# The length-64 stage of a Fourier filter as four 64x64 tiles, with VectorE adding and subtracting mirrored inputs

## The chip, the cores and the metric

The kernel runs on one core of one Trainium2 chip. The metric is the device time of one execution in microseconds (us), median of several runs. The core's engines are TensorE (PE in the profile, its weight loads PEld), VectorE (DVE), ScalarE (ACT), GpSimd (POOL) and SyncE (SP), which here only issues DMAs. All data are float32.

## The reference

```python
def _attn_ref(x, filt_r, filt_i):            # x: (8, 3008, 256), filters: (1505, 256)
    X = np.fft.rfft(x, axis=1)
    F = (filt_r + 1j * filt_i)[None, :, :]
    Y = X * F
    return np.fft.irfft(Y, n=x.shape[1], axis=1).astype(np.float32)

def _moe_ref(x, w_tok1, w_tok2, w_ch1, w_ch2):   # d_tok 256, d_ch 1536
    xt = x.transpose(0, 2, 1)
    h = np.maximum(xt @ w_tok1, 0.0) @ w_tok2
    u = x + h.transpose(0, 2, 1)
    h2 = np.maximum(u @ w_ch1, 0.0) @ w_ch2
    return (u + h2).astype(np.float32)
```

The second function is applied to what the first returns. Each of the 8 batches goes through the filter along its 3008 positions and then through the mixer.

## The kernel before, in words

**The filter.** 3008 = 47 x 64. A transform along 3008 is done as transforms of length 64 (the "a" stage), then of length 47 with the multiplication by the filter and the way back (stages "b", "m", "i"). Positions are folded: one half of the 128 partitions holds the rows n1 = 23, 22, ... 0, the other half the mirrored rows 24 to 46 (and row 0 shifted by one), each with its 64 values n2. `a_unit` (L470) multiplies one chunk of two such row pairs, a 128x512 tile, by the 128x128 table `wa`: one matmul, which the profile shows as two records, since a float32 matmul is two instructions. ScalarE copies the result from the bank to a tile `t1`, and a DMA writes it to the DRAM buffer `z_tmp`. A batch has 12 such chunks. `x_load` (L439) brings the input chunks into the filter's tiles `filts`, which are free in this stage, six chunks ahead. `t2_load` (L527) reads z back, 2 DMAs for each of 16 steps c; `b_pair` (L577) and `bi_pair` (L591) are the two matmuls of a step, each through `four` (L569), which issues four matmuls on 64x64 tiles of the array, one on each quarter. Between them VectorE multiplies by the filter (L583) and joins the two halves (L588, L589). The result goes to `g_tmp` in DRAM.

**The groups.** Batches are filtered in `GROUPS` (0), (1, 2), (3, 4), (5, 6), (7). Group 0 runs ahead of everything in a form of its own. Each later group runs beside the mixer of the batches of the group before it.

**The mixer.** `mix` (L893) goes over 288 items: 8 batches, 6 column blocks m, 6 pairs of hidden blocks jp. The channel products are done with seven multiplications in place of eight (Strassen-Winograd), hence many sums on VectorE. The order of one item is written out by hand. On TensorE: `up_first` (4 matmuls, L783), part 0 of `down` for the item before (3, L817), `up_last` (3, L799), part 1 of `down` for the item before (4, L817). On VectorE: `up_middle`, `h_sums` of the item before, the two sums of `up_last`; all of these are recorded under L761. ScalarE copies `s` (L786) and applies ReLU (L804). At jp 3 and 4 come the quarters of the next block's U (L682, L704), at jp 0 to 2 the steps of `finish`, which read the banks `po`, turn the block and store it through GpSimd's queue (L864). At item 32 of each batch's 36 the token sums of the next batch are formed (L660), from `g_tmp` tiles that are loaded once that batch's filter is done.

**Where the filter's steps go.** `mix` yields three times per item: place 0 between part 0 of `down` and `up_last`, place 1 between `up_last` and part 1 of `down`, place 2 at the end. In the loop at L1045 a table says at which yields the filter goes a step on. For the groups from (3, 4) on, a step of stage "a" is due at places 1 and 2 of every item. Then a `b_pair` is due at jp 2 and 5. Every engine works through its own instructions in the order in which they are issued.

**Banks.** Two PSUM banks, `acc` and `b`, are shared by `a_unit`, `b_pair`, `bi_pair`, the quarters of U and the token sums; `free_bank` hands them out in turn, `two_banks` takes both.

Of the kernel before, what the change touches and what calls it, by code (L numbers as in the profile page):

```python
# [55 lines left out]
def _make_tables():  # L56
    n2 = np.arange(N2)
    one, two = slice(0, HALF), slice(HALF, P)
    wa = np.zeros((P, K2, 4))
    wai = np.zeros((K2, 4, P))  # L60
    for k2 in range(K2):
        th, th1 = (2 * np.pi * ((n * k2) % N2) / N2 for n in (n2, n2 + 1))
        c, s, c1, s1 = np.cos(th), np.sin(th), np.cos(th1), np.sin(th1)
        alt, alt1 = 1.0 - 2.0 * (n2 % 2), 2.0 * (n2 % 2) - 1.0
        rows = ((c, c1), (-s, s1), (-s, -s1), (c, -c1)) if k2 else ((c, c1), (alt, alt1), (c, -c1), (alt, -alt1))
        for g, (plus, minus) in enumerate(rows):
            wa[one, k2, g], wa[two, k2, g] = plus, minus
        wai[k2] = wa[:, k2].T * (2.0 if k2 else 1.0)
    wa, wai = wa.reshape(P, P), wai.reshape(P, P)

    n1 = A - 1 - np.arange(A)
    wb = np.zeros((4, A, K2, P))
    wi = np.zeros((P, K2, 4, A))
    for k2 in range(K2):
        for s in range(2 * A):
            if s < A:
                k, sign, q = k2 + 64 * s, 1.0, s
            else:
                j = s - A + 1
# [12 lines left out]
            for g, to, w in parts:  # L92
                wb[g, :, k2, to] = w * np.where(n1 == 0, 0.5, 1.0)
                wi[to, k2, g] = w * (1.0 if k2 or edge else 2.0) / N
    f = np.float32
    wi = wi.reshape(P, K2, KR)
    wa0 = wa.reshape(P, K2, 4).transpose(0, 2, 1).reshape(P, P)
    wbi0 = np.zeros((4, K2, K2, P + KR))
    wbi0[:, 0:A, :, 0:P] = wb
    wbi0 = wbi0.reshape(P, K2, P + KR)  # L100
    wbi0[:, :, P:] = wi
    wb = wb.reshape(KR, K2, P)
    wbi = np.zeros((P, K2 // KC, 4, HALF))
    for h in range(2):
        r, to = slice(h * HALF, h * HALF + KH), slice(h * HALF, (h + 1) * HALF)
        for i in range(KC):
            wbi[r, :, i] = wb[h * KH:(h + 1) * KH, i::KC, to]
            wbi[i * HALF:(i + 1) * HALF, :, 2 + h, 0:KH] = wi[to, i::KC, h * KH:(h + 1) * KH]
    return wa.astype(f), wa0.astype(f), wai.astype(f), wbi.astype(f), wbi0.astype(f)


@with_exitstack
def kernel(
# [10 lines left out]
):  # L124
    nc = tc.nc

    wa_np, wa0_np, wai_np, wbi_np, wbi0_np = _make_tables()
    wa_d = nc.inline_tensor(wa_np, name="wa_t").ap()
    wai_d = nc.inline_tensor(wai_np, name="wai_t").ap()
    ident_d = nc.inline_tensor(np.eye(P, dtype=np.float32), name="ident_t").ap()  # L130
    wait_d = nc.inline_tensor(np.ascontiguousarray(wai_np.T), name="wait_t").ap()
# [3 lines left out]


    place_of = {b: (g, i) for g, bs in enumerate(GROUPS) for i, b in enumerate(bs)}
    z_d, g_d = ([nc.dram_tensor("%s_tmp%d" % (what, g), (K2, KR, len(bs), D), FP32, kind="Internal").ap()
                 for g, bs in enumerate(GROUPS)] for what in "zg")

    w2_d = nc.dram_tensor("w2_tmp", (MT, P, 7, 256), FP32, kind="Internal").ap()

# [31 lines left out]
        return turn[0]  # L174

    wa = glob.tile([P, P], FP32, name="wa")
    wai = glob.tile([P, P], FP32, name="wai")
    wai_t = glob.tile([P, P], FP32, name="wai_t")
    ident = h1p.tile([P, P], FP32, tag="h1", name="ident")
# [256 lines left out]

    xs, ahead = {}, []

    def x_load(b, c, i, queue=None):  # L439

        where, tag = ((t3p, "t3"), (tp, "t"), (vp, "v"), (up, "u"), (t1p, "t1"), (t2p, "t2"), (wbp, "wb"))[c // 2 if b == 0 else 6]
        xc, dc = (2 * XC, D // 2) if b == 0 else (XC, D)
        d0, c = divmod(c, A // xc)
        j = i - XB if b in GROUPS[1] else i
        if b and j >= 0:
            j %= XF
            t = filts[j // 2][:, j % 2]
        else:
            t = where.tile([P, xc, dc], FP32, tag=tag, name="x")

        def rows(n1, ap):
            xb = x[b]
            return bass.AP(tensor=xb.tensor, offset=xb.offset + n1 * D + d0 * dc, ap=ap + [[1, dc]])

        for h in range(2):
            n = xc - 1 if h and (c + 1) * xc == A else xc
            q = queue or (nc.gpsimd if b == 0 and h else nc.sync)
            q.dma_start(t[h * HALF:(h + 1) * HALF, 0:n, :],
                        rows(A + c * xc if h else A - 1 - c * xc, [[N1 * D, N2], [D if h else -D, n]]))
            if n < xc:  # L460

                q.dma_start(t[HALF:P - 1, n, :], rows(N1, [[N1 * D, N2 - 1]]))
                q.dma_start(t[P - 1:P, n, :], rows(0, [[N1 * D, 1]]))
        xs[b, c + d0 * (A // xc)] = t

    def rows_of(t_d, b):
        g, i = place_of[b]
        return t_d[g].rearrange("k (g a) b d -> (k g) a b d", a=A)[:, :, i, :]

    def a_unit(b, c):  # L470
        ps = bank(free_bank())
        nc.tensor.matmul(ps, wa0 if b == 0 else wa, xs.pop((b, c)).rearrange("p a d -> p (a d)"), start=True, stop=True)  # L472
        if b == 0:
            d0, c = divmod(c, NXC // 2)
            nc.scalar.copy(out=turned[:, ts(c, 2 * XC), ds(d0 * P, P)], in_=ps.rearrange("p (a d) -> p a d", d=P))
            return
        t1 = t1p.tile([P, XC, D], FP32, tag="t1", name="t1")
        nc.scalar.copy(out=t1.rearrange("p a d -> p (a d)"), in_=ps)
        (nc.scalar if b in GROUPS[1] else nc.sync).dma_start(rows_of(z_d, b)[:, ts(c, XC), :], t1)

    def dft(bs):
        first = bs[0] == 0
        nb = len(bs)
        todo = [(b, c) for b in bs for c in range(NXC)]
        wbs = {}

        def table_load(c):
# [12 lines left out]

        def more(n, queue=None):
            for i, u in to_load[0:n]:
                x_load(*u, i, queue)
            del to_load[0:n]

        more(NXC if first else XB if bs == GROUPS[1] else XF)
        if bs == GROUPS[1]:
            ahead.append(more)
        if not first:
            yield "a"  # L510
        for i, u in enumerate(todo):
            if first and i in (0, 2):
                w_load(i // 2)
            if first and i in (6, 8):
# [12 lines left out]
        def t2_load(c):  # L527
            if first:
                return
            t2s[c] = t2p.tile([P, KC, nb, D], FP32, tag="t2", name="t2")  # L530
            for h in range(2):
                nc.sync.dma_start(t2s[c][ds(h * HALF, KH)],
                                  z_d[place_of[bs[0]][0]][ts(c, KC), ts(h, KH)].rearrange("k r b d -> r k b d"))

        def b_unit(k):
            ps = bank("pg").rearrange("p (b d) -> p b d", b=2)[:, 0:nb, :]
# [29 lines left out]

        def four(outs, stat, mov):  # L569
            for i in range(2):  # L570
                for j in range(2):
                    nc.tensor.matmul(outs(i, j), stat(i, j), mov(i, j), start=True, stop=True)  # L572

        def both(half, n=HALF):
            return slice(half * HALF, half * HALF + n)

        def b_pair(c):  # L577
            pss, wb, t2 = two_banks(), wbs[c], t2s[c]
            four(lambda h, i: pss[h][both(i)], lambda h, i: wb[both(h, KH), i], lambda h, i: t2[both(h, KH), i])
            where = (p1p, p2p)  # L580
            for h in range(2):
                prods[c, h] = where[h].tile([P, 2, nb, D], FP32, tag="p%d" % (h + 1), name="p%d" % (h + 1))
# [7 lines left out]

        def bi_pair(c):  # L591
            pss, wb, p = two_banks(), wbs[c], prods.pop((c, 0))
            four(lambda i, h: pss[i][both(h)], lambda i, h: wb[both(i), 2 + h], lambda i, h: p[both(i), h])
            t3 = t3p.tile([P, KC, nb, D], FP32, tag="t3", name="t3")
            for i in range(KC):
                by_block(t3[:, i], pss[i])
            for h in range(2):
                nc.sync.dma_start(g_d[place_of[bs[0]][0]][ts(c, KC), ts(h, KH)].rearrange("k r b d -> r k b d"),
                                    t3[both(h, KH)])

        for c in range(FB):
            if not first:
# [373 lines left out]
    with tc.manual_schedule():  # L976
# [6 lines left out]
        for i, _ in enumerate(dft(GROUPS[0])):  # L983
# [4 lines left out]
            if i < NXC:  # L988
                if i in (1, 3, 5, 7, 9):
                    start()  # L990
                if i == NXC - 1:
                    copies()
                    for t, src in ((wa, wa_d), (wai, wai_d), (ident, ident_d)):
                        nc.scalar.dma_start(t, src)
            elif k >= 0:
                if k == K2 - 5:
# [48 lines left out]
        for b, i, place in mix(next_ready):  # L1045
# [8 lines left out]
                continue  # L1054
            jp = i % JP
            if coming in "aw":
                due = group == 0 or place > 0
            elif group:
                due = (jp, place) in {"b": ((5, 1), (2, 1)), "m": ((0, 0), (3, 0)), "i": ((1, 0), (3, 2))}[coming]
            else:  # L1060
# [34 lines left out]
```

## Time and profile before

| | us |
|---|---|
| median of 3 runs | 2509.74 (2509.21 to 2513.75) |
| the profiled execution | 2507.99 |
| its span | 2506.2 |

| group of instructions | count | mean ns |
|---|---|---|
| L472 matmul of stage "a", 128*128, 128x512 | 164 | 592 |
| L572 matmul of `four`, 64*64, 64x512 | 384 | 624 |
| L817, L783, L799 matmuls of the mixer, 128x256 | 6,720 | 379 to 389 |
| L588, L589 VectorE sums, SBUF to SBUF, 128x512 | 96 | 688 to 695 |
| L583 VectorE product with the filter, 128x1024 | 96 | 1210 |
| L478 ScalarE copy of z, 128x512 | 84 | 574 to 582 |

The page gives each engine's busy time and share of the span, the chain of work that ended last, and groups of instructions by line with their mean length. [...] matmuls overlap, so what one costs is the distance from its start to the next one's start. The timeline lists instructions in order of time, merged where they are alike; "x2" is the number of records, and a bracket gives the idle time of the engine before the line and what ended it.

### The profile page before, as it was taken

The page shows a single profiled execution, that of the slowest core. Times are in us where ns is not written, and L with a number is a line of the kernel's source. Part 1 is how long each engine was busy: PE and PEld are TensorE (multiplying, and loading weights), DVE is VectorE, ACT ScalarE, POOL GpSimd, SP SyncE. Part 2 cuts the span into 40 slices and gives each one's busy share as a digit, 9 for nine tenths or more (in the row PEclk, how much of TensorE's full clock was granted, in tenths as well). Part 3 has the DMA queues.
Part 4 walks back from the last instruction along what each step waited for, and adds up shares of the span by engine and source line. Part 5 has one row for each costly group of instructions (what it writes and reads, how often), then busy time and mean ns, then how long its engine had stood idle before and what let it go on. Part 6 is the DMA issues. An engine that isn't in the chain of part 4 may idle for free.

```text
span 2506.2 us, 33323 instructions
## 1 busy us (share of the span) xinstructions
PE 2434.7 (97%) x11716; PEld 1982.6 (79%) x11716; DVE 1811.4 (72%) x3344; ACT 681.6 (27%) x1348; POOL 601.2 (24%) x1086
## 2 busy tenths in 40 slices
PE   7978999999999999999999999999999999999997
PEld 4656776977788777888778877898888888898887
DVE  7786878566785878565785788756786678757776
ACT  5633322132221222223221222213222222212221
POOL 6573332112111211211121112111212111212121
PEclk8999999999999999999999999999999999999999
DMA  9974444354332331235332222314222122201100
GB/s 220 256 211 116 130 124 137 98 162 133 99 85 53 81 82 49 87 115 160 101 88 67 79 73 69 102 51 129 76 85 74 47 71 66 63 24 28 39 16 18
DMA packets 172479, 235.97 MB, mean 94 GB/s; under 512 B 32386, under 2 KB 122742, under 8 KB 172312
## 3 DMA queue, kind: packets, MB, share of 16 engines
q1 hardware_dynamic: 127848, 175.53, 24.8%
q0 software_dynamic: 33376, 48.46, 7.7%
q10 hardware_dynamic: 11088, 9.85, 1.3%
q8 instruction: 93, 1.52, 0.3%
q14 instruction: 74, 0.61, 0.1%
HBM read 156.49 MB, written 77.22 MB: 93 GB/s over the span
## 4 chain that ended last, share of the span: by engine, by line
PE 82%; DVE 12%; issue 2%; DMA 2%; ACT 1%; DVEq 0%; SPq 0%; ACTq 0%; POOL 0%; POOLq 0%
PE ps_po L817 29%; PE ps_pg L783 17%; PE ps_pg L799 12%; PE ps_b L660 3%; PE ps_acc L660 3%; PE ps_b L572 3%; DVE t L761 3%; PE ps_b L704 3%; PE ps_acc L704 2%; DVE p L583 2%; DVE hh L761 2%; PE ps_b L682 2%; PE ps_acc L682 2%; DVE s L761 1%; PE ps_b L472 1%
## 5 line engine op out<-in xcount | busy, mean ns | idle before, releaser
L864 POOL DMA_DIRECT2D out_dram<-r x757 | 412.5, 553 | 1607.5 <-ACT hh L804 1332.3
L761 DVE TENSOR_TENSOR hh<-ps_pg,s 128x512 f32<-128x512 f32 (+3 forms) x864 | 482.5, 586 | 431.3 <-ACT s L786 428.0
L804 ACT ACTIVATE hh<-hh 128x512 f32<-128x512 f32 (+1 forms) x576 | 347.9, 621 | 983.0 <-DVE hh L761 983.0
L817 PE MATMUL ps_po<-t,wc 128*128 128x256 f32 (+1 forms) x2304 | 543.5, 379 | 3.9 <-DVE t L761 3.1
L817 PEld LDWEIGHTS ps_po<-t,wc 128*128 128x128 f32 x2304 | 428.8, 190 | 121.7 <-DVE t L761 33.8
L783 PE MATMUL ps_pg<-v,wc 128*128 128x256 f32 (+1 forms) x1728 | 415.1, 376 | 2.7 <-DVE v L761 2.1
L817 PE MATMUL ps_po<-hh,wc 128*128 128x256 f32 (+1 forms) x1728 | 413.7, 375 | 0.2 <-ACT hh L804 0.2
L783 PEld LDWEIGHTS ps_pg<-v,wc 128*128 128x128 f32 x1728 | 327.7, 191 | 44.3 <-DVE v L761 5.9
L817 PEld LDWEIGHTS ps_po<-hh,wc 128*128 128x128 f32 x1728 | 328.9, 191 | 38.0 <-ACT hh L804 0.5
L799 PE MATMUL ps_pg<-u,wc 128*128 128x256 f32 (+1 forms) x1152 | 295.7, 379 | 5.0 <-DVE hh L761 5.0
L799 PEld LDWEIGHTS ps_pg<-u,wc 128*128 128x128 f32 x1152 | 215.3, 190 | 63.0 <-DVE hh L761 29.0
L761 DVE TENSOR_TENSOR t<-t,hh 128x256 f32<-128x256 f32 (+1 forms) x576 | 246.6, 428 | 19.8
L761 DVE TENSOR_TENSOR s<-ps_pg,hh 128x512 f32<-128x512 f32 (+1 forms) x288 | 196.1, 681 | 30.7 <-DVE hh L761 0.9
L761 DVE TENSOR_TENSOR t<-hh 128x512 f32<-128x512 f32 (+1 forms) x288 | 193.7, 673 | 0.6 <-ACT hh L804 0.6
L783 PE MATMUL ps_pg<-u,wc 128*128 128x256 f32 (+1 forms) x576 | 173.9, 384 | 13.5 <-DVE hh L761 13.5
L786 ACT COPY s<-ps_pg 128x256 f32<-128x256 f32 (+1 forms) x288 | 106.0, 368 | 284.1 <-PE ps_pg L783 282.2
L799 PE MATMUL ps_pg<-v,wc 128*128 128x256 f32 (+1 forms) x576 | 168.7, 375 | 0.0
L783 PEld LDWEIGHTS ps_pg<-u,wc 128*128 128x128 f32 x576 | 105.7, 190 | 64.1 <-DVE hh L761 36.5
L799 PEld LDWEIGHTS ps_pg<-v,wc 128*128 128x128 f32 x576 | 109.3, 190 | 12.5
L761 DVE TENSOR_TENSOR u<-ps_b,u 128x512 f32<-128x512 f32 (+3 forms) x107 | 61.7, 577 | 69.7 <-PE ps_b L704 65.0
L761 DVE TENSOR_TENSOR u<-ps_acc,u 128x512 f32<-128x512 f32 (+3 forms) x103 | 58.9, 572 | 57.2 <-PE ps_acc L704 52.0
L660 PE MATMUL ps_b<-t,w 128*128 128x256 f32 x384 | 83.9, 380 | 5.3 <-DVE p L583 4.7
(135 smaller groups left out, 2435.8 us busy)
## 6 DMA issues: line engine op xcount, KB each, us to landing
w<-w_tmp SPq DMA_DIRECT2D x35, 896.0 KB
out_dram<-r POOLq DMA_DIRECT2D x698, 32.0 KB, 2.6
t<-g_tmp SPq DMA_DIRECT2D x42, 512.0 KB
filt<-in_x_dram SPq DMA_DIRECT2D x145, 128.0 KB
t<-z_tmp SPq DMA_DIRECT2D x96, 192.0 KB
g_tmp<-t SPq DMA_DIRECT2D x96, 192.0 KB
z_tmp<-t SPq DMA_DIRECT2D x60, 256.0 KB
wb<-wbi_t SPq DMA_DIRECT2D x64, 128.0 KB
```

Source lines behind the costliest of these rows:

```text
L572: nc.tensor.matmul(outs(i, j), stat(i, j), mov(i, j), start=True, stop=True)
L583: nc.vector.tensor_tensor(out=prods[c, h], in0=pss[h].unsqueeze(1).to_broadcast([P, 2, nb, D]), in1=filts[c % FB][:, :, 0, :].unsqueeze(2) ...
L660: nc.tensor.matmul(acc[:, t, :], w1[:, a, ts(t, P)], t4[b, a // TC4][:, a % TC4, :], start=(a == 0 and t == 0), stop=(a == A - 1 and t == ...
L682: nc.tensor.matmul(ps[:, ds(q * P, n)], t4[b, c][:, r, ts(dh, P)], wai[:, 0:n], start=(first and q == 0), stop=(not first and q == 3))
L704: nc.tensor.matmul(ps[:, ds(j * hw, hw)], h1[:, n, :], w2m[m % 2][:, at, 0:hw], start=(i < 2 and j == 0), stop=(j == len(todo) - 1))
L761: nc.vector.tensor_tensor(out=out, in0=in0, in1=in1, op=op)
L783: nc.tensor.matmul(ps[:, 0:hw], chan[0][:, jp, n, :], mov, start=True, stop=True)
L786: nc.scalar.copy(out=s[:, 0], in_=g[0][:, 0, 0:hw])
L799: nc.tensor.matmul(ps[:, 0:hw], chan[0][:, jp, n, :], mov, start=True, stop=True)
L804: nc.scalar.activation(out=hs, in_=hs, func=AF.Relu)
L817: nc.tensor.matmul(po[i][:, j, 0:hw], chan[1][:, jp, n, :], mov, start=(jp == 0 and first == 1), stop=(jp == JP - 1 and last == 1))
L864: q.dma_start(bass.AP(tensor=ob.tensor, offset=ob.offset + row * D + g * cw, ap=[[N1 * D, 32], [D if h else -D, n], [1, cw]]), blocks[ts(g ...
```

## The change

From the third batch on (`tiled`, groups (3, 4), (5, 6) and (7)) stage "a" works on pairs of chunks. `x_pair` loads a pair so that the rows and their mirrored rows lie on the same partitions, with 6 DMAs (7 for the last pair of a batch) into one whole tile of `filts`; the first half of the partitions has the pair's first chunk, the second half its second. `x_sums` lets VectorE form sum and difference of the two, 128x512 each, into the tiles that `b_pair` later uses for its products. `a_pair` multiplies them by the new table `was` (two 64x64 halves, on both halves of the partitions) with `four`, and `z_out` copies both banks and stores them. The sums are formed one step ahead of their matmuls. A batch has 6 pairs. A step is now due once per item, at place 1. The z buffer has a new order of rows in all groups but the first, so `wa`'s columns are ordered anew and `t2_load` reads with 4 DMAs per step, 6 in step 0. Group 1, batches 1 and 2, keeps `a_unit`.

```diff
+    wa = wa.reshape(P, K2, 4)
+    by_sum = np.zeros((P, 2, 2, K2))
+    for e in range(2):
+        for h in range(2):
+            by_sum[:, e, h, 0] = wa[:, 0, 2 * e + h]
+            by_sum[:, e, h, 1:] = wa[:, 1:, 2 * h + e]
+    wa = by_sum.reshape(P, P)
+    return wa.astype(f), np.concatenate((wa[one], wa[one])).astype(f), wa0.astype(f), wai.astype(f), wbi.astype(f), wbi0.astype(f)
...
+    was = glob.tile([P, 2, HALF], FP32, name="was")
...
+    def x_pair(b, c, i, queue=None):
+
+        q = queue or nc.sync
+        t = filts[i % FB]
+        xb = x[b]
+
+        def rows(row, ap):
+            return bass.AP(tensor=xb.tensor, offset=xb.offset + row * D, ap=ap + [[1, D]])
+
+        for h in range(2):
+            a, to = 2 * XC * c + XC * h, slice(h * HALF, (h + 1) * HALF)
+            q.dma_start(t[to, 0], rows(A - 1 - a, [[N1 * D, N2], [-D, XC]]))
+            q.dma_start(t[h * HALF + 1:(h + 1) * HALF, 1], rows(A + a, [[N1 * D, N2 - 1], [D, XC]]))
+            n = min(XC, A - 1 - a)
+            q.dma_start(t[h * HALF:h * HALF + 1, 1, 0:n], rows(A + a + N1 * (N2 - 1), [[N1 * D, 1], [D, n]]))
+            if n < XC:
+                q.dma_start(t[h * HALF:h * HALF + 1, 1, n], rows(0, [[N1 * D, 1]]))
+        xs[b, c] = t
...
+    def z_out(b, ps, c, q):
         t1 = t1p.tile([P, XC, D], FP32, tag="t1", name="t1")
         nc.scalar.copy(out=t1.rearrange("p a d -> p (a d)"), in_=ps)
-        (nc.scalar if b in GROUPS[1] else nc.sync).dma_start(rows_of(z_d, b)[:, ts(c, XC), :], t1)
+        g, i = place_of[b]
+        q.dma_start(z_d[g][:, ts(c, XC), i, :], t1)
+
+    def x_sums(b, c, i):
+        t = xs.pop((b, c)).rearrange("p s a d -> p s (a d)")
+        where = (p1p, p2p)[i % 2]
+        sd = where.tile([P, 2, XC * D], FP32, tag="p%d" % (1 + i % 2), name="sd")
+        for e, op in enumerate((ALU.add, ALU.subtract)):
+            nc.vector.tensor_tensor(out=sd[:, e], in0=t[:, 0], in1=t[:, 1], op=op)
+        return sd
+
+    def a_pair(b, c, sd):
+        pss = [bank(tag) for tag in turn]
+        four(lambda h, e: pss[h][half_of(e)], lambda h, e: was[half_of(h), e], lambda h, e: sd[half_of(h), e])
+        for h in range(2):
+            z_out(b, pss[h], 2 * c + h, nc.sync)
 
     def dft(bs):
         first = bs[0] == 0
         nb = len(bs)
-        todo = [(b, c) for b in bs for c in range(NXC)]
+        tiled = bs not in GROUPS[0:2]
+        todo = [(b, c) for b in bs for c in range(NXC // 2 if tiled else NXC)]
...
-        more(NXC if first else XB if bs == GROUPS[1] else XF)
+        more(NXC if first else FB if tiled else XB)
         if bs == GROUPS[1]:
             ahead.append(more)
         if not first:
             yield "a"
+        if tiled:
+            sd = x_sums(*todo[0], 0)
+            yield "a"
         for i, u in enumerate(todo):
+            if tiled:
+                now, sd = sd, x_sums(*todo[i + 1], i + 1) if i + 1 < len(todo) else None
+                more(1)
+                a_pair(*u, now)
+                yield "a" if i + 1 < len(todo) else "w"
+                continue
...
             for h in range(2):
-                nc.sync.dma_start(t2s[c][ds(h * HALF, KH)],
-                                  z_d[place_of[bs[0]][0]][ts(c, KC), ts(h, KH)].rearrange("k r b d -> r k b d"))
+                z = z_d[place_of[bs[0]][0]].rearrange("(e h k) a b d -> e h a k b d", e=2, h=2)
+                for e in range(2):
+                    to = t2s[c][ds(h * HALF + e * A, A)]
+                    k = c == 0
+                    if k:
+                        nc.sync.dma_start(to[:, 0:1], z[h, e, :, 0:1])
+                    nc.sync.dma_start(to[:, k:KC], z[e, h, :, c * KC + k:c * KC + KC])
...
-                    for t, src in ((wa, wa_d), (wai, wai_d), (ident, ident_d)):
+                    for t, src in ((wa, wa_d), (was, was_d), (wai, wai_d), (ident, ident_d)):
                         nc.scalar.dma_start(t, src)
...
             if coming in "aw":
-                due = group == 0 or place > 0
+                due = place == 1 or group == 0
```

`four` is unchanged and moved out of `dft`, with `both` renamed to `half_of`.

More of the change, by code (lines that the diff above doesn't have):

```diff
@@ L108, in _make_tables @@
             wbi[i * HALF:(i + 1) * HALF, :, 2 + h, 0:KH] = wi[to, i::KC, h * KH:(h + 1) * KH]
-    return wa.astype(f), wa0.astype(f), wai.astype(f), wbi.astype(f), wbi0.astype(f)
+    wa = wa.reshape(P, K2, 4)
[6 more added lines that the diff above has]
+    return wa.astype(f), np.concatenate((wa[one], wa[one])).astype(f), wa0.astype(f), wai.astype(f), wbi.astype(f), wbi0.astype(f)
 @with_exitstack
@@ L125 @@
     nc = tc.nc
-    wa_np, wa0_np, wai_np, wbi_np, wbi0_np = _make_tables()
+    wa_np, was_np, wa0_np, wai_np, wbi_np, wbi0_np = _make_tables()
     wa_d = nc.inline_tensor(wa_np, name="wa_t").ap()
+    was_d = nc.inline_tensor(was_np, name="was_t").ap()
     wai_d = nc.inline_tensor(wai_np, name="wai_t").ap()
@@ L137 @@
     place_of = {b: (g, i) for g, bs in enumerate(GROUPS) for i, b in enumerate(bs)}
-    z_d, g_d = ([nc.dram_tensor("%s_tmp%d" % (what, g), (K2, KR, len(bs), D), FP32, kind="Internal").ap()
-                 for g, bs in enumerate(GROUPS)] for what in "zg")
+    z_d, g_d = ([nc.dram_tensor("%s_tmp%d" % (what, g), shape + (len(bs), D), FP32, kind="Internal").ap()
+                 for g, bs in enumerate(GROUPS)] for what, shape in (("z", (P, A)), ("g", (K2, KR))))
     w2_d = nc.dram_tensor("w2_tmp", (MT, P, 7, 256), FP32, kind="Internal").ap()
@@ L443, in x_load @@
         d0, c = divmod(c, A // xc)
-        j = i - XB if b in GROUPS[1] else i
+        j = i - XB
         if b and j >= 0:
@@ L468, in rows_of, with four, half_of @@
         return t_d[g].rearrange("k (g a) b d -> (k g) a b d", a=A)[:, :, i, :]
+    def four(outs, stat, mov):
+        for i in range(2):
+            for j in range(2):
+                nc.tensor.matmul(outs(i, j), stat(i, j), mov(i, j), start=True, stop=True)
+    def half_of(half, n=HALF):
+        return slice(half * HALF, half * HALF + n)
     def a_unit(b, c):
@@ L476, in a_unit @@
             return
+        z_out(b, ps, c, nc.scalar)
+    def z_out(b, ps, c, q):
         t1 = t1p.tile([P, XC, D], FP32, tag="t1", name="t1")
         nc.scalar.copy(out=t1.rearrange("p a d -> p (a d)"), in_=ps)
-        (nc.scalar if b in GROUPS[1] else nc.sync).dma_start(rows_of(z_d, b)[:, ts(c, XC), :], t1)
+        g, i = place_of[b]
[12 more added lines that the diff above has]
+            z_out(b, pss[h], 2 * c + h, nc.sync)
     def dft(bs):
@@ L502, in more @@
             for i, u in to_load[0:n]:
-                x_load(*u, i, queue)
+                (x_pair if tiled else x_load)(*u, i, queue)
             del to_load[0:n]
-        more(NXC if first else XB if bs == GROUPS[1] else XF)
+        more(NXC if first else FB if tiled else XB)
         if bs == GROUPS[1]:
@@ L565, in two_banks @@
             return [bank(tag).rearrange("p (b d) -> p b d", b=2)[:, 0:nb, :] for tag in turn]
[L569 to L575, printed above, removed]
         def b_pair(c):
             pss, wb, t2 = two_banks(), wbs[c], t2s[c]
-            four(lambda h, i: pss[h][both(i)], lambda h, i: wb[both(h, KH), i], lambda h, i: t2[both(h, KH), i])
+            four(lambda h, i: pss[h][half_of(i)], lambda h, i: wb[half_of(h, KH), i], lambda h, i: t2[half_of(h, KH), i])
             where = (p1p, p2p)
@@ L592, in bi_pair @@
             pss, wb, p = two_banks(), wbs[c], prods.pop((c, 0))
-            four(lambda i, h: pss[i][both(h)], lambda i, h: wb[both(i), 2 + h], lambda i, h: p[both(i), h])
+            four(lambda i, h: pss[i][half_of(h)], lambda i, h: wb[half_of(i), 2 + h], lambda i, h: p[half_of(i), h])
             t3 = t3p.tile([P, KC, nb, D], FP32, tag="t3", name="t3")
@@ L598, in bi_pair @@
                 nc.sync.dma_start(g_d[place_of[bs[0]][0]][ts(c, KC), ts(h, KH)].rearrange("k r b d -> r k b d"),
-                                    t3[both(h, KH)])
+                                    t3[half_of(h, KH)])
         for c in range(FB):
```

## The prediction

> **What bounds the kernel now.** I read the page first. TensorE is busy for 97% of the span and carries 82% of the chain that ended last, VectorE 12%.
>
> ```profile
> PE 2434.7 (97%) x11716; PEld 1982.6 (79%) x11716; DVE 1811.4 (72%) x3344; ACT 681.6 (27%) x1348; POOL 601.2 (24%) x1086
> ...
> PE 82%; DVE 12%; issue 2%; DMA 2%; ACT 1%; DVEq 0%; SPq 0%; ACTq 0%; POOL 0%; POOLq 0%
> ```
>
> A share over the span says little about 60 matmuls, so I asked for the three stretches that change: the length-64 stage of batches 3 and 4 (502 to 603 us), of 5 and 6 (1096 to 1197) and of 7 (1690 to 1740). In the table by stretches TensorE is busy 52.00 of 52.00 us in 560:612, 105.00 of 105.00 in 1095:1200 and 52.00 of 52.00 in 1690:1742, at a granted clock of 1.00. There is no gap to hide in: what leaves TensorE there leaves the time, unless a new wait fills it. Now the price of the piece, in the timeline of TensorE (start, length, line, tiles, count):
>
> ```profile
> 601.72 0.59 PE L799 MATMUL ps_pg<-v,wc 128*128 128x256 f32 x2
> 602.15 1.02 PE L472 MATMUL ps_acc<-filt,wa 128*128 128x512 f32 x2
> 603.01 1.89 PE L817 MATMUL ps_po<-t,wc 128*128 128x256 f32 x8
> ```
>
> Matmuls overlap, so I read starts, not lengths: one `a_unit` occupies 602.15 to 603.01. Its two records start 0.429 us apart, in all 60 units. The new form is not foreign to this trace. `four` already runs in `b_pair` and `bi_pair` (L572):
>
> ```profile
> 614.82 0.59 PE L799 MATMUL ps_pg<-v,wc 128*128 128x256 f32 x2
> 615.35 0.65 PE L572 MATMUL ps_acc<-t,wb 48*64 48x512 f32 x2
> 615.36 0.65 PE L572 MATMUL ps_b<-t,wb 48*64 48x512 f32 x2
> 615.83 0.59 PE L572 MATMUL ps_acc<-t,wb 48*64 48x512 f32 x2
> 615.84 0.60 PE L572 MATMUL ps_b<-t,wb 48*64 48x512 f32 x2
> 616.36 1.99 PE L817 MATMUL ps_po<-t,wc 128*128 128x256 f32 x8
> 618.20 0.59 PE L783 MATMUL ps_pg<-u,wc 128*128 128x256 f32 x2
> ```
>
> The four tiles do run together (pairs start 0.01 us apart), but not for free. From 615.35 to 616.36 are 1.01 us. The entry starts 0.09 late (614.82 plus two steps of 0.216 is 615.25), and the eight matmuls of L817 behind it take 1.84 where they take 1.72 elsewhere. Together about 1.21 us. The L572 group on 64*64 tiles, which is the exact shape of the new one, takes the same 1.01 from start to next start (625.20 to 626.21).
>
> **TensorE's gain.** Two `a_unit`s cost 4 x 0.429 = 1.72 us, one `a_pair` 1.21. There are 5 batches x 6 pairs = 30: 30 x (1.72 - 1.21) = 15.3 us. Here a rule speaks against the change. The row: leaving and entering the full array costs about 0.2 us of the 1.21. The Trainium skill, "TensorEngine Tiling (Array Packing)", section Tiling Modes, says that tiles work independently, but that a change of tiling mode drains TensorE. By the first half alone four tiles of 512 columns take the time of one `a_unit`, 0.86, and 30 pairs would save 25.7 us; by the row, which contains both changes of mode, 15.3. I take the row.
>
> **VectorE's new work.** 60 additions of 128x512 from SBUF. The nearest rows are L588 and L589 (`p<-p,p` 128x512), means 688 and 695 ns, which start 0.605 apart when they follow one another. That is 60 x 0.605 = 36 us more occupancy, more than TensorE gains, so the question is where it lies. `x_sums` is emitted at place 1 of an item, behind the two sums of `up_last` and ahead of the next item's `up_middle`. That is where VectorE waits for TensorE now (last bracket: idle before it, and who ended it):
>
> ```profile
> 574.69 1.29 DVE L761 TENSOR_TENSOR hh<-ps_pg,s 128x512 f32<-128x512 f32 x2
> 579.89 0.42 DVE L761 TENSOR_TENSOR hh<-ps_pg,s 128x256 f32<-128x256 f32 x1 [3.91 <-ACT s L786]
> ```
>
> By place in the cycle of six items the idle time before `up_middle` is 2.43 us at jp 0, 0.52 at jp 1, 2.56 at jp 2, 2.61 at jp 3, 3.91 at jp 4 and 1.49 at jp 5 (behind another gap of 3.21). With two sums of 1.21 together, and TensorE faster by 0.51, about 0.7 to 2.2 us are left at jp 0, 2, 3 and 4. At jp 5 the sums fall into the 3.21. Those sums are hidden. Two places are not.
>
> At jp 0 `finish` follows at place 2:
>
> ```profile
> 602.01 1.28 DVE L761 TENSOR_TENSOR hh<-ps_pg,s 128x512 f32<-128x512 f32 x2
> 603.21 0.68 DVE L761 TENSOR_TENSOR u<-ps_po,u 128x512 f32<-128x512 f32 x1
> 604.91 0.42 DVE L761 TENSOR_TENSOR r<-ps_po,r 128x256 f32<-128x256 f32 x1 [1.02 <-ACT r L829]
> 605.25 1.01 DVE L761 TENSOR_TENSOR u<-ps_po,u 128x512 f32<-128x512 f32 x2
> 606.18 0.41 DVE L761 TENSOR_TENSOR r<-ps_po,r 128x256 f32<-128x256 f32 x1
> 606.51 0.41 DVE L761 TENSOR_TENSOR hh<-ps_pg,s 128x256 f32<-128x256 f32 x1
> ```
>
> Call T the end of `up_last` on TensorE (602.15). The sums run to T+2.35, the first `u` to T+2.95. ScalarE copies two z tiles (0.57 each) behind its ReLUs and only then `r`, so the second `r` sum starts near T+3.36, `up_middle` at T+4.96, and its last read is over at T+6.2. TensorE wants the next `up_last` at T+1.21+1.72+1.72+1.29 = T+5.95. That is 0.25 us, with the weight load behind it 0.35, at 5 items with jp 0: 1.7 us. At jp 4 `four` needs both spare banks, and VectorE reads the quarter of U in one of them until 583.69, while `up_last` ends at 583.55: some 0.15 us at 5 items, 0.7 us. Together 2.4 us.
>
> Hidden, with their cover: ScalarE's copies are as many as before, 12 a batch, and ScalarE is 27% busy. SyncE issues 6 loads and 2 stores per step where it issued 4 and 2, about 0.64 and 0.5 us each, 5 of a step's 7.2 us. A load has two items (some 14 us) from its issue to `x_sums`, against a median landing of 4.5. If that cover fails, VectorE stands at the head of its queue for a DMA, and `up_middle`, `h_sums` and so TensorE wait behind it. The first steps have 18 loads ahead, issued from about 494.5; the first pair should land by 503, and its sums are due at about 507. One step per item instead of two moves the first `b_pair` three items later, which still ends before the batch's token sums (item 63 of 72; the sums are at 68). GpSimd's memsets of the filter tiles now queue behind 16 output stores (8.7 us), but the filter then has three items, some 27 us, where it had 9.
>
> **The new layout of z, for all groups.** `t2_load` issues 4 DMAs instead of 2, 6 for c 0. SyncE waits mostly for buffers in steady state, so this is hidden, except at the start of batches 1 and 2, where the path already ends in DMA:
>
> ```profile
> 239.28 0.65 PE L572 MATMUL ps_b<-t,wb 48*64 48x512 f32 x2 [1.21 <-DMA wb<-wbi_t]
> ```
>
> There `t2_load(0)` stands ahead of the tables and the filter on SyncE, and VectorE waits 4.63 us for that filter. Four more DMAs at 0.4 us each (the L532 pair takes 0.80) delay it by 1.6 us. The stall before L572 p there is 2.75 us now and the clock of that stretch 0.96, so up to 4 if the clock drops further; nothing if `wb` were late for another reason. I take 2.0. The table `was` adds one issue on ScalarE at the start, 0.45 us, under its wait of 1.0 for the filter: 0, at most 0.4.
>
> **Sum.** -15.3 + 2.4 + 2.0 = -10.9 us. Against the profiled execution (2507.99, span 2506.2) that is 2497.1; the median of the three runs is 1.75 higher, so 2498.8. Predicted: 2499 us.
>
> **Rivals.**
> 1. Everything is hidden, at the start too: -15.3, 2494.4. For it: no stalls at all in these stretches now. Against: the walk at jp 0 has no slack. Chance 0.2.
> 2. Waits eat much of it: 0.3 us in every second item of the three stretches (15 x 0.3 = 4.5), 1.5 us of late filter at each first `b_pair`, 4 at the start of batch 1: -15.3 + 4.5 + 4.5 + 4 = -2.3, 2507.4. For it: the stretches with `b_pair`, whose VectorE load is like the new one, lose 0.2 to 0.4 us a cycle to "DVE hh". Against: that is per six items, and the new stretches have lighter single blocks. Chance 0.14.
> 3. VectorE becomes the bound: the sums lie on the path, +36.3 - 15.3 + 2 = +23, 2533. It decides from the point where over (15.3 - 2)/36.3 = 37% of their time is exposed, which needs loads that land late or slack that isn't there. Against: five of six idle gaps above exceed 1.21 + 0.51 in sum with the gap next to them. Chance 0.03.
>
> My forecast (2496.5 to 2503) has the remaining 0.63. About 0.2%, 5 us, is what a measurement of this kernel can tell from no change: 2504.7 to 2514.8 is the same. Of rival 2 most is inside that, of the forecast's upper tail little: faster 0.86, same 0.11, slower 0.03. The range of 8 in 10 takes in rival 1 and part of rival 2: 2493.5 to 2505.5.
>
> **What would show it.** The new line of `four` with `sd,was` 64*64 64x512, eight records per step, 1.2 us from the matmul ahead to the end of its trace in L817; 60 sums of 128x512 with hardly any idle time before them, none of it for a DMA; the three stretches free of TensorE gaps over 0.4 us; L572's first wait at 2.8 instead of 1.21. I am wrong if `four` takes over 1.4 us on this data, if sums wait for x, or if up_last waits on VectorE at jp other than 0 and 1.

## The result and the profile after

The changed kernel takes 2499.35 us (median of 5 runs, 2497.13 to 2500.53) against 2509.63: ratio 0.9955, 95% interval 0.994 to 0.9969. Predicted were 2499 us. The sum was right; two of its terms were not where I had put them. The lines have new numbers after the change: L783 is L844, L799 is L860, L817 is L878, L572 is L501, L761 is L822, L583 is L644, L588 is L649; L526 is `x_sums`, L517 the copy in `z_out`, L765 the quarters of U. In some of the experiments they shift again by a few lines.

The busy times on the page of the changed kernel:

```profile
PE 2420.1 (97%) x11836; PEld 1962.4 (79%) x11836; DVE 1846.7 (74%) x3404; ACT 678.6 (27%) x1348; POOL 598.4 (24%) x1086
```

TensorE has 120 matmul records more (30 x 8 for 60 x 2) and is busy 14.6 us less. VectorE has 60 instructions and 35.3 us more. The chain of work that ended last could be followed back over half the span only, so its shares are not to be set beside those of before. What can be compared is the start of every item of the mixer on TensorE (items count from 0 to 287, and jp is the number modulo 6). With the time from one item to another, in the profiled executions:

| stretch | before | after |
|---|---|---|
| start to item 36 (mixer of batch 1 begins) | 496.1 | 500.2 |
| items 36 to 53: stage "a" of batches 3 and 4 | 147.49 | 139.63 |
| items 54 to 95 | 345.49 | 345.95 |
| items 96 to 107 | 101.33 | 103.42 |
| items 108 to 125: stage "a" of 5 and 6 | 147.49 | 139.63 |
| items 126 to 179 | 446.47 | 449.37 |
| items 180 to 191: stage "a" of 7 | 94.84 | 90.64 |
| items 192 to 251 | 471.11 | 472.73 |
| rest | 255.90 | 255.95 |

The stages themselves gain 7.86, 7.86 and 4.20 us. Part of that is only lent: the filter's later steps come three items later, so steps with tiles leave the end of one stretch and enter the next (+0.46 and +2.09, +2.90, +1.62). The balance of the three groups is -12.85 us. The start lost 4.2 in this pair of profiles; over all profiles, below, it is 1.9 with ranges that overlap.

In the stage, the timeline of TensorE (start, length, line, tiles) at jp 0 now reads:

```profile
550.48 0.59 PE L860 MATMUL ps_pg<-v,wc 128*128 128x256 f32 x2
551.00 0.65 PE L501 MATMUL ps_acc<-sd,was 64*64 64x512 f32 x2
551.01 0.65 PE L501 MATMUL ps_b<-sd,was 64*64 64x512 f32 x2
551.48 0.60 PE L501 MATMUL ps_acc<-sd,was 64*64 64x512 f32 x2
551.49 0.59 PE L501 MATMUL ps_b<-sd,was 64*64 64x512 f32 x2
552.02 1.99 PE L878 MATMUL ps_po<-t,wc 128*128 128x256 f32 x8
553.85 0.59 PE L844 MATMUL ps_pg<-u,wc 128*128 128x256 f32 x2
```

It is the picture of the old `four` to within 0.01 us: 0.09 late, 1.02 from 551.00 to 552.02, and 1.83 for the eight matmuls behind where they take 1.73 elsewhere. And VectorE beside it:

```profile
550.77 1.28 DVE L822 TENSOR_TENSOR hh<-ps_pg,s 128x512 f32<-128x512 f32 x2
551.97 1.28 DVE L526 TENSOR_TENSOR sd<-filt 128x512 f32<-128x512 f32 x2
553.17 0.69 DVE L822 TENSOR_TENSOR u<-ps_po,u 128x512 f32<-128x512 f32 x1
554.02 0.42 DVE L822 TENSOR_TENSOR r<-ps_po,r 128x256 f32<-128x256 f32 x1 [0.17 <-ACT r L890]
554.37 1.01 DVE L822 TENSOR_TENSOR u<-ps_po,u 128x512 f32<-128x512 f32 x2
555.29 0.42 DVE L822 TENSOR_TENSOR r<-ps_po,r 128x256 f32<-128x256 f32 x1
555.62 0.42 DVE L822 TENSOR_TENSOR hh<-ps_pg,s 128x256 f32<-128x256 f32 x1
```

The two sums (L526) stand without a gap behind the sums of `up_last`, never behind a DMA, and fill what was a wait of 1.02 us for `r` before.

At the start of batches 1 and 2, first on TensorE, then on VectorE:

```profile
243.31 0.71 PE L501 MATMUL ps_b<-t,wb 48*64 48x512 f32 x2 [1.93 <-DMA filt<-in_filt_r_dram]
...
252.70 1.62 PE L501 MATMUL ps_b<-p,wb 64*64 64x512 f32 x3 [3.05 <-DVE p L649]
```

```profile
249.47 1.23 DVE L644 TENSOR_TENSOR p<-ps_b,filt 128x1024 f32<-128x1024 f32 x1 [5.96 <-DMA wb<-wbi_t]
```

The waits that were 1.21, 2.75 and 4.63 us are 1.93, 3.05 and 5.96.

### The profile page after: what moved, and what is told of

It reads as the page before. It is cut to its first block, busy times and chain, and to the rows that moved or that the text cites. A ratio compares the mean times of both kernels' runs of the same rounds, so it can differ in the third digit from the quotient of the medians.

```text
span 2497.6 us, 33945 instructions
## 1 busy us (share of the span) xinstructions
PE 2420.1 (97%) x11836; PEld 1962.4 (79%) x11836; DVE 1846.7 (74%) x3404; ACT 678.6 (27%) x1348; POOL 598.4 (24%) x1086
## 4 chain that ended last, share of the span: by engine, by line
PE 44%; DVE 5%; issue 1%; DMA 0%; ACT 0%; DVEq 0%; POOL 0%; SPq 0%; ACTq 0%; POOLq 0%
PE ps_po L878 17%; PE ps_pg L844 10%; PE ps_pg L860 7%; PE ps_b L721 2%; PE ps_acc L721 2%; PE ps_b L765 2%; PE ps_acc L765 2%; DVE t L822 1%; DVE hh L822 1%; PE ps_acc L501 1%; DVE p L644 1%; PE ps_b L501 1%; PE ps_b L743 1%; PE ps_acc L743 1%; DVE s L822 1%
## 5 line engine op out<-in xcount | busy, mean ns | idle before, releaser
L822 DVE TENSOR_TENSOR hh<-ps_pg,s 128x512 f32<-128x512 f32 (+3 forms) x864 | 482.6, 586 | 390.2 <-ACT s L847 386.8
L878 PE MATMUL ps_po<-t,wc 128*128 128x256 f32 (+1 forms) x2304 | 546.6, 380 | 4.2 <-DVE t L822 3.1
L878 PEld LDWEIGHTS ps_po<-t,wc 128*128 128x128 f32 x2304 | 426.3, 190 | 132.4 <-DVE t L822 41.1
L844 PE MATMUL ps_pg<-v,wc 128*128 128x256 f32 (+1 forms) x1728 | 415.5, 377 | 2.1 <-DVE v L822 2.1
L878 PE MATMUL ps_po<-hh,wc 128*128 128x256 f32 (+1 forms) x1728 | 413.5, 375 | 0.2 <-ACT hh L865 0.2
L844 PEld LDWEIGHTS ps_pg<-v,wc 128*128 128x128 f32 x1728 | 327.8, 191 | 43.5 <-DVE v L822 5.9
L878 PEld LDWEIGHTS ps_po<-hh,wc 128*128 128x128 f32 x1728 | 329.1, 191 | 38.2 <-ACT hh L865 0.5
L860 PE MATMUL ps_pg<-u,wc 128*128 128x256 f32 (+1 forms) x1152 | 295.8, 379 | 6.0 <-DVE hh L822 6.0
L860 PEld LDWEIGHTS ps_pg<-u,wc 128*128 128x128 f32 x1152 | 215.5, 190 | 63.7 <-DVE hh L822 30.5
L822 DVE TENSOR_TENSOR t<-t,hh 128x256 f32<-128x256 f32 (+1 forms) x576 | 245.2, 426 | 19.9
L822 DVE TENSOR_TENSOR s<-ps_pg,hh 128x512 f32<-128x512 f32 (+1 forms) x288 | 196.1, 681 | 30.3 <-DVE hh L822 0.5
L822 DVE TENSOR_TENSOR t<-hh 128x512 f32<-128x512 f32 (+1 forms) x288 | 192.9, 670 | 0.6 <-ACT hh L865 0.6
L844 PE MATMUL ps_pg<-u,wc 128*128 128x256 f32 (+1 forms) x576 | 173.8, 383 | 14.0 <-DVE hh L822 14.0
L860 PE MATMUL ps_pg<-v,wc 128*128 128x256 f32 (+1 forms) x576 | 168.8, 375 | 0.0
L844 PEld LDWEIGHTS ps_pg<-u,wc 128*128 128x128 f32 x576 | 105.6, 190 | 51.6 <-DVE hh L822 37.0
L860 PEld LDWEIGHTS ps_pg<-v,wc 128*128 128x128 f32 x576 | 109.3, 190 | 12.6
L822 DVE TENSOR_TENSOR u<-ps_b,u 128x256 f32<-128x256 f32 (+2 forms) x102 | 58.3, 572 | 67.5 <-PE ps_b L765 61.8
L822 DVE TENSOR_TENSOR u<-ps_acc,u 128x512 f32<-128x512 f32 (+2 forms) x108 | 62.4, 577 | 56.5 <-PE ps_acc L765 52.2
```

The costliest lines, as they stand in the source:

```text
L822: nc.vector.tensor_tensor(out=out, in0=in0, in1=in1, op=op)
L844: nc.tensor.matmul(ps[:, 0:hw], chan[0][:, jp, n, :], mov, start=True, stop=True)
L860: nc.tensor.matmul(ps[:, 0:hw], chan[0][:, jp, n, :], mov, start=True, stop=True)
L878: nc.tensor.matmul(po[i][:, j, 0:hw], chan[1][:, jp, n, :], mov, start=(jp == 0 and first == 1), stop=(jp == JP - 1 and last == 1))
```

## The experiments

The theory: TensorE gains 0.50 us per pair, VectorE's sums are hidden, and the new layout of z costs a little at one place, the start of batches 1 and 2. Against it: the gain comes from the schedule, the sums cost, or the reads of z cost everywhere. Beside the experiments the kernel before had medians from 2509.14 to 2510.68 us, so a difference between two experiments' totals is uncertain by about 1 us; the stretches are the finer measure.

**The layout alone (e1_layout).** The new z and its reads, with `a_unit`, the old loads and two steps per item for every group:

```diff
...
-        tiled = bs not in GROUPS[0:2]
+        tiled = False
...
-                due = place == 1 or group == 0
+                due = group == 0 or place > 0
```

The parts left out give `a_unit`'s loads and stores their old numbers and queues.

> Only the new order of z and its reads (4 DMAs per step, 8 in step 0): all groups keep a_unit, two steps per item. My theory: the layout costs only at the start of batches 1 and 2, 1.6 to 2.0 us: 2511.5 us against 2509.6. Rival A: the extra reads cost 0.2 us in each of the 64 steps: about 2522. Rival B: part of the gain came with the layout: below 2508.

Measured: 2510.59 us beside 2510.04 for the kernel before, ratio 1.0002 (0.9994 to 1.001). From item 36 on its stretches agree with before to 0.3 us each (147.49, 345.46, 101.31, ...). The extra reads cost nothing in the steps, and the layout brings nothing by itself. Rivals A and B fall. The 1.6 to 2.0 at the start can't be told from zero by this time alone.

**Full matmuls in place of the tiles (e2_full).** The sums are formed, but go through 128x128 matmuls with `wa`, so another result is computed:

```diff
-        four(lambda h, e: pss[h][half_of(e)], lambda h, e: was[half_of(h), e], lambda h, e: sd[half_of(h), e])
+        for h in range(2):
+            nc.tensor.matmul(pss[h], wa, sd[:, h], start=True, stop=True)
```

> The changed kernel with the four 64x64 tiles of a pair replaced by two 128x128 matmuls of the same 512 columns (the result is then another one); sums, loads, copies and schedule stay. My theory: TensorE's term of the sum comes back, 30 x 0.50 = 15 us: 2514. Rival: the gain came from the new schedule (one step per item, paired loads), not from the tiles: 2497 to 2501.

Measured: 2514.04 us, 14.7 over the changed kernel and 1.0014 (1.0006 to 1.0021) times before. The stages take 145.96, 145.96 and 93.80, that is 6.33, 6.33 and 3.16 more than with tiles, 15.8 together. The tiles carry the whole gain; sums, loads and the new schedule with full matmuls are slightly slower than before. Over all stretches from item 36 on they lose 2.8 us against before, and the items show where: the five at jp 4 take 12.06 against 11.70, and each group's second item takes 6.38 where one without filter work takes 6.04.

**Without the sums (e3_no_sums).** The tiles get the loaded rows; the 60 additions and subtractions are left out:

```diff
-        where = (p1p, p2p)[i % 2]
-        sd = where.tile([P, 2, XC * D], FP32, tag="p%d" % (1 + i % 2), name="sd")
-        for e, op in enumerate((ALU.add, ALU.subtract)):
-            nc.vector.tensor_tensor(out=sd[:, e], in0=t[:, 0], in1=t[:, 1], op=op)
-        return sd
+        return t
...
+                a_pair(*u, now)
                 more(1)
-                a_pair(*u, now)
```

A step's tiles are issued ahead of the next loads here, since they now read the loaded tile itself.

> The changed kernel without VectorE's 60 sums: the tiles are fed with the loaded rows (the result leaves out the sums). My theory: the sums are hidden, at most 1 us is gained: 2498 to 2499.5; the 0.2 us at jp 4 and the 0.34 us in each group's second item stay, since they don't come from the sums. Rival: the sums cost several us somewhere, and removing 36 us of VectorE work gains over 3: below 2496.

Measured: 2498.72 us (2496.59 to 2500.41), ratio to before 0.9957 (0.9944 to 0.9969), the same as the changed kernel's. Its stages take 139.95, 139.93 and 90.78, even 0.1 to 0.3 longer than with the sums (it lies in the items at jp 4, where the tiles of the two banks start 0.13 us apart and the set takes 1.24 in place of 1.02; why is open). In 497:611 VectorE is busy 76.70 us instead of 91.17, TensorE 113.75 instead of 113.64. The sums cost nothing that can be seen. The items at jp 4 (11.57 and 11.55, with the sums 11.40) and each group's second item (6.38 in both) are no shorter without them, so what is lost there isn't theirs.

**The sums twice (e4_double_sums).**

```diff
-        for e, op in enumerate((ALU.add, ALU.subtract)):
+        for e, op in 2 * ((0, ALU.add), (1, ALU.subtract)):
```

> The changed kernel with each pair of sums done twice, 36 us more of VectorE. My theory: the idle time left before up_middle (0.17 us after sums at jp 0, 0.6 at jp 1, 0.7 at jp 5, over 1.2 elsewhere) takes most of it; about 1.0 + 0.4 + 0.3 us are exposed per cycle, five cycles, 5 to 9 us: 2504 to 2508. If VectorE were already the bound: 2535. If it had slack to spare everywhere: 2499.

Measured: 2505.99 us, 6.6 over the changed kernel, ratio to before 0.9984 (0.9976 to 0.9991). The stages grow by 2.95, 2.96 and 1.58. 36 us more work make 7.5, so four fifths of a second pair of sums are still hidden, and the rest fits my range. Where the cover ends is seen in the items: those at jp 1, 2 and 3 grow by 0.26 to 0.66 us, those at jp 0, 4 and 5 keep their 7.26, 11.40 and 7.26.

**The tiles twice (e5_two_fours).**

```diff
-        four(lambda h, e: pss[h][half_of(e)], lambda h, e: was[half_of(h), e], lambda h, e: sd[half_of(h), e])
+        for _ in range(2):
+            four(lambda h, e: pss[h][half_of(e)], lambda h, e: was[half_of(h), e], lambda h, e: sd[half_of(h), e])
```

> The changed kernel with the four tiles of each pair computed twice, back to back. If the entry into tiles and the way back (0.09 and 0.10 us) are what a pair costs beyond its columns, the second set costs 0.86 to 1.02 us, 30 times, 26 to 31 us: 2525 to 2530. If each set pays all of it again: 1.22 x 30 = 37 us, 2536.

Measured: 2523.04 us, ratio to before 1.0058 (1.0045 to 1.0072), 23.7 over the changed kernel and 2 us below my range. The total's difference includes the chance of the start; the stages grow by 10.30, 10.30 and 5.14, which is 0.86 for each of the 30 second sets. The timeline of TensorE, from the first set to the matmuls behind the second:

```profile
552.54 0.65 PE L501 MATMUL ps_acc<-sd,was 64*64 64x512 f32 x2
...
553.02 0.59 PE L501 MATMUL ps_acc<-sd,was 64*64 64x512 f32 x2
...
553.45 0.60 PE L501 MATMUL ps_acc<-sd,was 64*64 64x512 f32 x2
...
553.88 0.60 PE L501 MATMUL ps_acc<-sd,was 64*64 64x512 f32 x2
...
554.42 1.99 PE L879 MATMUL ps_po<-t,wc 128*128 128x256 f32 x8
```

Once in tiles, a set of four runs at the full rate of its columns: 0.86, the time of one `a_unit`. A visit of one set costs 1.217 (an item with it takes 7.26, one without filter work 6.04), so coming and going cost 0.36 us, not the 0.2 that I had read from the edges. The rest is seen in the starts: the first half-set takes 0.48 and the last 0.54, those between 0.43. It fits the drain at a change of tiling mode of which the Trainium skill speaks ("TensorEngine Tiling (Array Packing)", section Tiling Modes); that the 0.36 us are this drain and nothing else, no run shows.

**Two steps per item (e6_two_steps).**

```diff
-                due = place == 1 or group == 0
+                due = group == 0 or place > 0
```

> The changed kernel with a filter step due at places 1 and 2 of every item, as before the change, in place of one per item. My theory: VectorE then has 2.4 us of sums in an item that leaves 0.2 to 2.2, and at jp 4 the tiles at place 2 wait for the quarters of U in both banks: 4 to 10 us slower than the change, 2503 to 2509. Rival: the schedule doesn't matter, TensorE's work is the same: 2498 to 2501.

Measured: 2527.27 us, ratio to before 1.0075 (1.0061 to 1.0089): 28 over the changed kernel, some three times the most that I had expected. TensorE's waits in 490:620 of this kernel (who waited, for whom, us in total, times, longest):

```profile
PE ps_acc L501 <- ACT t L517: 2.3, 3, 1.0
PE ps_pg L860 <- DVE hh L822: 1.7, 2, 1.2
PE ps_acc L501 <- DVE u L822: 1.5, 2, 0.8
PE ps_b L501 <- DVE u L822: 1.0, 1, 1.0
```

The second set of tiles needs both banks while ScalarE still copies the first one's z out of them (L517), or VectorE reads U from them. VectorE's work on `hh` and `t`, of which I thought first, has 2.4 of the 7.7 us of waits there. ScalarE was not late by work of its own. Its waits in the same stretch hold one that I had not thought of, and that the changed kernel does not have in its stage:

```profile
ACT t L517 <- DMA z_tmp<-t: 13.7, 8, 3.6
```

There are two tiles `t1`, and with two pairs in an item a copy of z waits until an earlier store has left its tile. The copy `s` stands behind it, and VectorE's `hh` once waits 3.92 us for that. How much of the 28 us comes by this way, no run separates. Where I was wrong for certain is the count: nearly every item of the stage pays (item 37 takes 10.56 and item 38 9.55, where two sets of tiles should bring 8.47). So the schedule is a condition of the gain, not its source: with the old table the change would have lost.

**Another start (e7_start, e9_before_start).** Step 0 of batches 1 and 2 gets its filter through GpSimd's queue, the table goes ahead of z, and the eight reads of z become six; in e9 the same start in the kernel before, without the last point:

```diff
-                    k = c == 0
+                    k = c == 0 and e != h
...
+                if bs == GROUPS[1] and c == 0:
+                    table_load(0)
+                    filt_pair(0, nc.gpsimd)
                 t2_load(c)
-                if not first:
+                if not first and (bs != GROUPS[1] or c):
                     w_load(c)
```

> The changed kernel with another start for batches 1 and 2: the filter of step 0 is issued on GpSimd's queue, the table ahead of z on SyncE, and step 0 reads z with 6 DMAs in place of 8. My theory: the wait for the filter before the first inverse step (3.05 us on TensorE, VectorE 5.96) goes, 2 to 4 us: 2495.5 to 2497.5. Rival: z itself is late, and nothing moves: 2499.

> The kernel before with the other start of batches 1 and 2 alone (filter of step 0 on GpSimd's queue, table ahead of z). My theory: both waits there (1.28 and 2.82 us on TensorE) go whatever the layout of z, 4 to 5 us: 2505; items 8 to 11 take 36.4 us as in the changed kernel with that start. Rival: the wait was made by the new layout's extra reads, and before gains under 2 us: 2508.

Measured: 2494.9 us (2491.71 to 2500.15), ratio to before 0.9942 (0.9928 to 0.9955); and 2507.71, ratio 0.9991 (0.9981 to 1.0). In both profiles TensorE's two waits there are gone, and items 8 to 11, which hold the place, take 36.44 and 36.36 us. The totals fit less well: e7 lies 0.6 us below its range, and e9 gains 3.0 us on the 2510.68 measured beside it, where the interval (0 to 4.8) leaves room for my theory's 4 to 5 and for the rival's 2. The profile decides: both waits are there in the kernel before and gone in e9, so the extra reads did not make them. One loss is left: the first four tiles do not run together there and take 1.98 and 1.90 us in place of 1.02. This is the TensorE timeline of e7_start at the first tiles of stage "i", which waited 3.05 us:

```profile
251.70 1.46 PE L881 MATMUL ps_po<-hh,wc 128*128 128x256 f32 x6
253.09 0.65 PE L501 MATMUL ps_b<-p,wb 64*64 64x512 f32 x2
```

**Before, twice more (e8_before_a, e10_before_b).** Unchanged, for their profiles.

> The kernel before once more, for a second profile of its first 250 us: items 8 to 11 of the mixer (start of the filter of batches 1 and 2) took 41.37 us in its first profile and 40.65 to 42.98 in seven kernels with the new layout of z. If the layout costs 1.6 us there, as I predicted, this shows about 39.5 and the first profile was an exception; if it costs nothing, 41 to 42. The time ahead of the mixer: near 143.4 if the new kernels' 146 to 149 is theirs, 144 to 150 if it is chance.

> The kernel before a third time, for the same two stretches: items 8 to 11 at about 39.5 us if the new layout costs what I predicted, 41 to 42 if it costs nothing; the time ahead of the mixer 143.4 or anywhere in 144 to 150.

Single times 2510.94 and 2507.99. Items 8 to 11 take 39.11 and 39.78 us, with 41.37 in the first profile and 39.65 in e12 below a mean of 40.0. The seven kernels with the new z and the old start took 40.65 to 42.98, mean 41.4. The layout's cost there is about 1.4 us by the means, but the ranges overlap, and the changed kernel's own profile was its worst case. Clearer is the wait ahead of the first tiles, from the end of the turn of the matmul before them: 1.2 to 1.5 us in the four profiles with the old z, 2.0 to 2.7 in the seven with the new. These tiles then take 1.3 to 2.2 us in place of 1.02, since the four no longer start together. The wait behind them goes the other way, 1.9 to 2.9 before and 0.1 to 3.2 with the new z. The time ahead of the mixer was 147.20 and 144.53.

**Where `was` is loaded (e11_start_was, e12_was_only).** Ahead of the mixer the kernels with `was` took 146.3 to 152.5, those without 143.3 to 147.2, so I tried the load by itself, late in e11 (with the other start), and as a useless table in the kernel before in e12:

```diff
-                    for t, src in ((wa, wa_d), (was, was_d), (wai, wai_d), (ident, ident_d)):
+                    for t, src in ((wa, wa_d), (wai, wai_d), (ident, ident_d)):
...
         ahead[0](XF, nc.gpsimd)
+        nc.gpsimd.dma_start(was, was_d.rearrange("p (e k) -> p e k", e=2))
```

> The changed kernel with the other start of batches 1 and 2, and the table `was` loaded after the weights, on GpSimd's queue, instead of at the start on ScalarE's. The time ahead of the mixer was 146.3 to 152.5 us in eight kernels with `was` at the start and 143.3 to 147.2 in four without. If `was` costs 3 us there: 143 to 146 ahead of the mixer, 2492 in all. If the difference is chance: 146 to 150, and 2495 in all, as with the other start alone.

> The kernel before with one more 64 KB table loaded where the change loads `was`, and never used. If that load costs 3 us: 146 to 150 us ahead of the mixer and 2513 in all. If it costs at most 0.4, as I predicted: 143 to 147 and 2510.

Measured: 2496.44 us, ratio 0.9951 (0.9939 to 0.9964), with 149.93 us ahead of the mixer though the load is gone; and 2508.75, ratio 0.9996 (0.9988 to 1.0005), with 146.49. `was` costs nothing that can be seen (the 146.49 alone lies in both expected ranges; the total decides). The start of this program varies by some us from run to run, and whether the changed kernel has a us or two of its own in it stays open: up to item 36 the four profiles with the old z and the old start (before, e8, e10, e12) have a mean of 497.0 us (496.0 to 499.0), the seven with the new z and the old start 498.9 (496.5 to 500.5). With these means the sum of the stretches is -12.85 + 1.9 = -10.95 us, beside -10.3 between the medians.

## Why the prediction was right, step by step

- **TensorE's price, right.** Predicted 1.72 against 1.21 us per pair, 15.3 in all. Measured 1.716 against 1.217, 15.0. By the ideal of the independent tiles it would have been 25.7; the row that contained the change of mode was the one to take, and e5 gives the visit its price, 0.36 us, 11 us in 30. My 0.2 for it was too small, which did no harm, since the sum took the visit as a whole.
- **VectorE's sums hidden, right.** e3 shows no cost of theirs, and e4 that most of a second pair would fit as well.
- **The 0.35 us at jp 0, wrong.** It was to be 1.7 us; items at jp 0 and the item behind them take 7.26 us, with no wait at all. The step that failed is "ScalarE copies two z tiles (0.57 each)": they follow one another in 0.47, so the sum on `r` began at T+3.11 and not T+3.36 (T is 550.91 here), and the next `up_last` came at T+5.96 with VectorE done at T+5.93. I had added lengths where I should have added distances from start to start, as I did on TensorE. On ScalarE:

```profile
552.62 0.57 ACT L517 COPY t<-ps_acc 128x512 f32<-128x512 f32 x1
553.09 0.59 ACT L517 COPY t<-ps_b 128x512 f32<-128x512 f32 x1
```

- **The 0.15 us at jp 4, right in kind.** TensorE waits 0.20 us for the bank at each of five items, 1.0 us in place of 0.7; in e3, without the sums, these items are no shorter, so the sums have no part in it. On TensorE, then VectorE, whose read of the quarter ends at 533.25 where the tiles were due at 533.19:

```profile
532.67 0.59 PE L860 MATMUL ps_pg<-v,wc 128*128 128x256 f32 x2
533.40 0.65 PE L501 MATMUL ps_acc<-sd,was 64*64 64x512 f32 x2
```

```profile
532.11 1.14 DVE L822 TENSOR_TENSOR u<-ps_acc,u 128x512 f32<-128x512 f32 x2
```

- **A wait that I had not seen.** Each group's second item forms sums but has no tiles yet. At jp 1 there part 1 of `down` now waits for `h_sums`, which an `a_unit` used to cover. On TensorE, then VectorE:

```profile
510.04 0.59 PE L860 MATMUL ps_pg<-v,wc 128*128 128x256 f32 x2
510.74 1.97 PE L878 MATMUL ps_po<-t,wc 128*128 128x256 f32 x8
```

```profile
509.91 0.68 DVE L822 TENSOR_TENSOR t<-hh 128x512 f32<-128x512 f32 x1
510.63 0.88 DVE L822 TENSOR_TENSOR t<-t,hh 128x256 f32<-128x256 f32 x2
```

  From 510.04 two matmuls end their turn at 510.47; the next start at 510.74, when `t` has come. With the weight load behind it that is 0.34 us, three times, 1.0 us. The removed work was cover, and I had asked only what the added work needs. This 1.0 and the jp 4 term's extra 0.3 took the place of the 1.7: 2.0 in all where I had 2.4. That the two misses nearly cancel is luck. 15.0 - 2.0 is 13.0; the table's balance is 12.85.
- **The start of batches 1 and 2, right in size, wrong in the working.** Predicted 2.0, about 1.4 by the means over profiles. The description of the change and the prediction count 6 reads of z in step 0 where the trace has 8 on SyncE; I had misread the nested loops. With six reads more in place of four, my own rate of 0.4 us would have made 2.4 of the 1.6. The wait ahead of the first tiles grew by about 1.0 in the means, less than either; the second one did not grow with it in every profile. That 2.0 came out near is in part luck.
- **Rivals.** That all is hidden missed the 2 us of waits. Rival 2's late filter at the first `b_pair` of the later groups did not occur. Rival 3 needed exposed sums; e3 excludes it.

## What to carry to other kernels

Price a change of array mode by the visit: 0.36 us here, so four 64x64 tiles of 512 columns (1.22 us) in place of two 128x128 matmuls (1.72) are worth it even singly, and a second set in the same visit costs only 0.86. When a piece of TensorE work shrinks, ask what it covered, item by item, and walk both queues by start-to-start distances. A matching schedule belongs to the change: the same tiles at the old places were 28 us slower.

## What the runs showed that I had not expected

From item 36 on, the stretches of the table repeat from profile to profile mostly to 0.1 us or better where their work is the same (stage "a" of batches 3 and 4 in the six profiles with the old form: 147.49 five times and 147.58 once; in after, e7 and e11: 139.63, 139.62 and 139.63); the kernels with the other start differ by up to 2.3 us in items 54 to 95. The time ahead of the mixer ranges from 143.3 to 152.5. There the DMA engines' busy share in the profiles before and after is 0.82 to 1.06, and the granted clock falls to 0.66 and 0.74 between 20 and 40 us; which of the two makes the time vary, or whether either does, stays open. A difference of 10 us is therefore better read by stretches than by the total. The best version tried is the changed kernel with the other start: 2494.9 us, 0.9942 (0.9928 to 0.9955) of the time before.
